# Six blocks of a sequence transform on two 64-row tiles of the array in place of the full 128 rows

## The chip, the cores and the metric

One core of a Trainium2 chip runs the kernel. The metric is the device time of one execution in microseconds. Three runs of the kernel before gave 882.68, 882.76 and 883.76 us, a median of 882.76 us. Operands are float32; a product is built up from rounded halves, as told below.

## The reference, cut to what matters

The input is a sequence of S = 2048 rows by D = 512. Two branches work on it, and a gate per row mixes them.

```
g = sigmoid((x * gate_w).sum(-1))
a = x @ dft_hid_re.T ;  b = x @ dft_hid_im.T
y = dft_seq_re @ a - dft_seq_im @ b                 # the sequence transform, 2048 x 2048 twice
o = windowed causal attention of x, 32 heads of 16, window 256
out = g * y + (1 - g) * (o @ wo)
```

The change lies in `y`, in its second half, the product with `dft_seq_im`.

## The kernel before, in words

**Precision.** The kernel keeps each operand of a large product as two tiles, `hi` (the value rounded to the format `F32R`) and `lo` (the rest, also `F32R`), and forms hi x hi, hi x lo and lo x hi (`TERMS`). A product of 128 x 128 weights with 128 x 512 data is therefore three matmuls, each with its own weights or its own data. The attention's value product, `pv` (L411), takes plain float32, and so do the two small products in `m_rows` and `l_rows` (L331, L343).

**The sequence transform.** `dense` is a generator that emits matmuls one by one. For each half (0 is the real one, 1 the imaginary one) and each block `tb` of 128 rows of the result it sums over 16 chunks of 128 rows of the sequence: 16 x 3 = 48 matmuls into one PSUM bank (`dc`, one of two banks of the pool `ps_d`). `c_block` (L447) runs such a block, and `c_chunk` (L442) emits the three matmuls of one chunk. The weights `w` are pieces of the transform's matrix, loaded as `raw` and split by VectorE into `hi` and `lo` (L82, L83); the data `ab` are the 16 tiles `big` of `a` or `b`. At the end of a block, `add_r` (L563 to L573) reads the first half's result `r` back, adds the bank times the gate on VectorE (L566), and, once the attention is over, calls `wo_block`.

**The output projection.** `wo_block` (L592) loads 128 rows of the attention's result, splits them (ScalarE L80 and VectorE L83), runs 12 matmuls (L604) into a bank `t` out of the four of `ps_a` (tag `st`), and adds that bank times 1 - g to `r` on VectorE (L606) ahead of the store of the output.

**The order.** TensorE runs in the order in which the code is written. During the attention, the main loop emits score and probability products and draws matmuls from `dense` between them (`fill`); the transform's blocks up to `tb` = 9 of the second half are emitted or begun that way. When the loop is over, `attention_done` loads `wo` and appends it to `FIN`, and `for _ in stream: pass` emits what is left. From there on each finished block calls `wo_block` twice, once for a block that was waiting and once for itself, so that six blocks of 48 transform matmuls (`tb` 10 to 15) alternate with 24 projection matmuls, and 48 projection matmuls stand at the end. The order on VectorE and ScalarE is set by a scheduler at build time.

**Tiles of the array.** A matmul whose output has 32 partitions runs on a tile of the array of 128 rows by 32 columns: that is so in `pv`, whose four products `p` go to four such tiles side by side, and in L331 and L343. The profile prints it as 128*32. All others run on 128*128.

Of the kernel before, what the change touches and what calls it, by code (L numbers as in the profile page):

```python
# [7 lines left out]
F32 = mybir.dt.float32  # L8
F32R = mybir.dt.float32r
AF = mybir.ActivationFunctionType  # L10
OP = mybir.AluOpType
# [3 lines left out]
P = 128  # L15
# [16 lines left out]
def fnet_window_mix(ctx: ExitStack, tc: tile.TileContext, xT, x, wqk, wv, wr, wi, cr, ci, wo, gw, out):  # L32
    nc = tc.nc
# [3 lines left out]
    st = ctx.enter_context(tc.tile_pool(name="st", bufs=3))  # L37
    ev = ctx.enter_context(tc.tile_pool(name="ev", bufs=5))
    at = ctx.enter_context(tc.tile_pool(name="at", bufs=2))
    ps_a = ctx.enter_context(tc.tile_pool(name="ps_a", bufs=4, space=PSUM))  # L40
    ps_o = ctx.enter_context(tc.tile_pool(name="ps_o", bufs=2, space=PSUM))
    ps_d = ctx.enter_context(tc.tile_pool(name="ps_d", bufs=2, space=PSUM))
# [11 lines left out]
    def ld(dst, src):  # L54
        return nc.sync.dma_start(dst, src)
# [38 lines left out]
    def load_raw(src):  # L94
        raw = st.tile([P, 1024], F32, name="raw", bufs=2)
        ld(raw, src)
        return raw

    def split_raw(raw, act=False):
        hi = st.tile([P, 1024], F32R, name="hi")  # L100
        lo = st.tile([P, 1024], F32R, name="lo")
        for c in HALVES:
            split(hi[:, c], lo[:, c], raw[:, c], act)
        return hi, lo
# [7 lines left out]
    def load_x(ss, j):  # L112
        raw = st.tile([P, 1024], F32, name="raw", bufs=2)
        ld(raw.rearrange("p (k s) -> p k s", k=2), xT[ss, 2 * j:2 * j + 2].rearrange("k p s -> p k s"))
        for c in range(2):
            XRAW[2 * j + c, ss] = raw[:, HALVES[c]]
# [41 lines left out]
    half = const.tile([P, 2], F32, name="half")  # L158
    mrow = const.tile([P, 2], F32, name="mrow")
    for t, edges in ((half, ((0, 16, 32, 48, 64, 80), (16, 32, 48, 64, 80, 96))), (mrow, ((96, 98), (98, 100)))):  # L160
        nc.gpsimd.memset(t, 0.0)
        for h in range(2):
            for i, e in enumerate(edges[h]):
                a = t[:, h:h + 1]
# [23 lines left out]
    g1 = const.tile([P, 16], F32, name="g1")  # L188
# [23 lines left out]
    TERMS = ((0, 0), (0, 1), (1, 0))  # L212
# [7 lines left out]
    def qk_first(w):  # L220
        pss = [ps_a.tile([P, 512], F32, name="s", tag="st") for _ in range(2)]
        for dk in range(DK):
            for i in range(2):
                c = dk * 256 + i * 128
                for n, (a, b) in enumerate(TERMS):
                    nc.tensor.matmul(pss[i], w[a][:, c:c + 128], XT[dk, 0][:, b],
                                     start=dk == 0 and n == 0, stop=dk == 3 and n == 2)
        for i in range(2):
            qk_evict(0, 0, i, pss[i])

    def qk_proj(g, ss, w):
        for i in range(2):
            ps = ps_d.tile([P, 512], F32, name="dqk", tag="d")
            n = 0
            for dk in range(DK):
                c = dk * 256 + i * 128
                for a, b in TERMS:
                    nc.tensor.matmul(ps, w[a][:, c:c + 128], XT[dk, ss][:, b],  # L238
                                     start=n == 0, stop=n == 11)
                    n += 1  # L240
                    if n < 12:
                        yield
            qk_evict(g, ss, i, ps)
            yield
# [21 lines left out]
    def v_proj(sb, w):  # L266
        ps = ps_d.tile([P, 512], F32, name="dv", tag="d")
        yield from row_proj(sb, w, ps)
        t = ev.tile([P, 512], F32, name="ev")
        mark("act", nc.scalar.copy(t, ps))  # L270
        store(v_scr[sb // 2][sb % 2].rearrange("r a g x -> r (a g x)"), t)
        yield
# [164 lines left out]
    SC = [*range(4, 16), *range(4)]  # L437

    def c_chunk(w, i, ab, ps):
        s8 = i % 8  # L440
        for a, b in TERMS:
            nc.tensor.matmul(ps, w[a][:, s8 * 128:(s8 + 1) * 128], ab[SC[i]][:, b],  # L442
                             start=i == 0 and a + b == 0, stop=i == 15 and a == 1)
            if i < 15 or a == 0:
                yield

    def c_block(get, half, tb, ab, done):  # L447
        ps = ps_d.tile([P, 512], F32, name="dc", tag="d")
        for i in range(16):
            if i % 8 == 0:  # L450
                w = get((half, tb * 2 + i // 8))
            yield from c_chunk(w, i, ab, ps)
        done(tb, ps)
        yield

    def c_pair(get, half, tb, ab, done, last=False):
# [18 lines left out]
    def late(fn, *args):  # L475
        with behind("act", "dve"):
            return fn(*args)

    def dense():
        wraw = [load_raw(wv[i]) for i in range(2)]  # L480
        qk_first(wq0)
        wvs = [split_raw(r, True) for r in wraw]
        load_x(1, 0)
        load_x(1, 1)
        yield
        for ss in range(4):
            if ss:
                yield from qk_proj(0, ss, wq0)
            for c in range(4):
                yield from v_proj(ss * 4 + c, wvs)  # L490
                have.add(("v", ss * 4 + c))
                if c == 1:
                    have.add(("qk", 0, ss))
                if ss < 3:
                    if c in (1, 2):
                        late(split_x, ss + 1, (2 * c - 2, 2 * c - 1), ss == 0)
                        if ss < 2:
                            load_x(ss + 2, c - 1)
                elif c == 0:
                    raw = load_raw(wqk[1])  # L500
                    wraw = [load_raw(wi[0])]
                elif c == 2:
                    w = late(split_raw, raw)
        for g in range(1, NG):
            for ss in range(4):
                yield from qk_proj(g, ss, w)
                have.add(("qk", g, ss))
                if g == 1:
                    if ss == 0:
                        wraw.append(load_raw(wi[1]))  # L510
                    elif ss < 3:
                        if ss == 1:
                            ws = []
                        ws.append(late(split_raw, wraw[ss - 1]))
                        if ss == 1:
                            raw = load_raw(wqk[2])
                        else:
                            gate_load(0)
                elif g == 2:
                    if ss == 0:  # L520
                        raw = load_raw(wqk[3])
                        wraw = [load_raw(wr[0])]
                    elif ss == 2:
                        nextw = late(split_raw, raw)
                        wraw.append(load_raw(wr[1]))
                elif ss in (0, 2):
                    if ss == 0:
                        ws = []
                    ws.append(late(split_raw, wraw[ss // 2]))
            if g == 1:  # L530
                for sb in range(16):
                    yield from ab_proj(1, sb, ws)
                    if sb == 1:
                        nextw = late(split_raw, raw)
                    if sb % 2 == 0 and sb < 14:
                        gate_load(sb // 2 + 1)
                    if sb % 2:
                        late(gate, sb - 1)
                        late(gate, sb)
            if g < 3:  # L540
                w = nextw
        ab = {}
        for sb in range(16):
            if sb >= 4:
                ab[sb] = big.tile([P, 2, 512], F32R, name="big")
            yield from ab_proj(0, sb, ws, ab.get(sb))
        for sc in range(4):
            ab[sc] = load_ab(0, sc)
        have.add("proj")
        def store_r(tb, ps):  # L550
            t = ev.tile([P, 512], F32, name="ev")
            nc.scalar.activation(t, ps, AF.Copy, scale=g1[:, tb:tb + 1])
            ld(r_scr[0][tb], t)

        get = c_pieces([*((0, k) for k in (*range(28), 28, 30, 29, 31)),
                        *((1, k) for k in (0, 2, 1, 3, *range(4, 32)))])
        for tb in range(14):
            yield from c_block(get, 0, tb, ab, store_r)
        yield from c_pair(get, 0, 14, ab, store_r, True)
        ab = nxt  # L560
        wait = []

        def add_r(tb, ps):  # L563
            r = ev.tile([P, 512], F32, name="ev")
            ld(r, r_scr[0][tb])
            nc.vector.scalar_tensor_tensor(r, ps, g1[:, tb:tb + 1], r, op0=OP.mult, op1=OP.add)  # L566
            if FIN:
                if wait:
                    wo_block(wait.pop(0))
                wo_block(tb, r)  # L570
            else:
                ld(r_scr[1][tb], r)
                wait.append(tb)  # L573

        yield from c_pair(get, 1, 0, ab, add_r)
        for tb in range(2, 16):
            yield from c_block(get, 1, tb, ab, add_r)
        while wait:
            wo_block(wait.pop(0))

    FIN = []
# [147 lines left out]
```

## Time and profile before

| What | Before |
|---|---|
| Runs, median (lowest to highest) | 882.76 us (882.68 to 883.76) |
| Span of the profiled execution, first to last instruction | 881.0 us |
| Between that span and the median of the runs | 1.76 us |
| Mean clock granted to TensorE | 0.998 of full |
| TensorE busy (matmuls) | 867.3 us |
| Matmuls of the transform (L442), all | 1536 |
| Projection matmuls (L604) | 192 |
| First of the six blocks behind the attention starts at | 772.51 us of the chain |

The profiled execution's own time is its span of 881.0 us with what lies around it; the page gives no other time for it, so the median of the runs stands for the whole. Times of rows are microseconds from the span's start. TensorE appears twice: PE is the matmuls, PEld the weight loads, which may run beside them. A matmul's record is longer than its share of the engine, since matmuls overlap: the pitch, from one start to the next, is what counts. In a row of the chain or the timeline stand the start, the length, the line, what is written and read, and how many instructions were merged.

### The profile page before, as it was taken

To read this page: it belongs to the slowest core of one execution; us is meant where nothing else is said; L and a number is where in the kernel's file an instruction comes from. 1 tells how busy PE (TensorE), PEld (TensorE's weight loads), DVE (VectorE), ACT (ScalarE), POOL (GpSimd) and SP (SyncE) were. 2 spreads that over 40 slices of the span, in tenths; PEclk is the share of its full clock that TensorE was granted. 3 is DMA by queue.
4 is the path that set the end of the run, shared out by engine and by line. 5 is a ranking of instruction groups with operands and counts; after the bars stand their busy time and mean duration, and the time that the engine had idled before them with its cause. 6 is when DMAs were issued, how large, how long until landed. Compare 5 with 4: busy or idle time off the path is not lost.

```text
span 881.0 us, 17206 instructions
## 1 busy us (share of the span) xinstructions
PE 867.3 (98%) x5184; PEld 690.6 (78%) x5184; DVE 604.8 (69%) x1965; ACT 590.3 (67%) x1794; POOL 384.9 (44%) x1069
## 2 busy tenths in 40 slices
PE   7999899999999999999999999999999999999998
PEld 5888677777777778787878787878777787788886
DVE  4688789777888678787877677778786433544342
ACT  5488789878889887888888878888786444101000
POOL 9100165554544446656456565745555665100000
PEclk9999999999999999999999999999999999999999
DMA  7877667675656126544444454469743424355453
GB/s 246 274 232 212 197 218 263 216 246 179 225 198 213 43 72 216 159 130 126 140 141 132 147 147 128 134 203 324 256 154 95 137 96 144 110 180 165 134 160 113
DMA packets 89822, 152.13 MB, mean 173 GB/s; under 512 B 26752, under 2 KB 35456, under 8 KB 89728
## 3 DMA queue, kind: packets, MB, share of 16 engines
q1 hardware_dynamic: 89728, 151.02, 54.6%
q8 instruction: 41, 0.67, 0.3%
q14 instruction: 53, 0.43, 0.2%
HBM read 103.81 MB, written 47.19 MB: 171 GB/s over the span
## 4 chain that ended last, share of the span: by engine, by line
PE 93%; DVE 2%; DMA 2%; ACT 1%; issue 0%; SPq 0%; ACTq 0%
PE dc L442 40%; PE s L319 9%; PE dab L260 9%; PE t L384 8%; PE dqk L238 8%; PE o L411 8%; PE t L604 5%; PE dv L260 5%; DMA qk_scr<-hl 1%; DMA pt<-xT 1%; DMA ab_scr<-hl 1%; DVE sm L321 1%; ACT sm L324 0%; PE s L343 0%; PE s L331 0%
## 5 line engine op out<-in xcount | busy, mean ns | idle before, releaser
L442 PE MATMUL dc<-big,hi 128*128 128x512 f32 x1024 | 341.0, 394 | 0.0
L390 POOL TENSOR_SCALAR_AFFINE_SELECT pt<-pt 64x128 f32<-64x128 f32 x512 | 195.4, 382 | 285.2 <-ACT pt L385 270.1
L321 DVE CUSTOM_DVE_ANT_0 sm<-s,mask 128x320 f32<-128x320 f32 (+4 forms) x512 | 232.6, 462 | 114.6 <-PE t L384 74.9
L324 ACT ACTIVATE sm<-sm,nm 128x320 f32<-128x320 f32 (+4 forms) x512 | 276.6, 541 | 25.8 <-DVE nm L321 21.7
L385 ACT ACTIVATE pt<-t 128x320 f32<-128x320 f32 (+4 forms) x512 | 210.8, 414 | 117.9 <-PE t L384 114.4
L442 PEld LDWEIGHTS dc<-big,hi 128*128 128x128 f32 x1024 | 189.4, 188 | 28.1
L442 PE MATMUL dc<-big,lo 128*128 128x512 f32 x512 | 201.6, 394 | 0.0
L384 PE MATMUL t<-ring,pad 128*128 128x320 f32 (+4 forms) x512 | 158.3, 309 | 3.8 <-ACT pad L302 2.8
L319 PE MATMUL s<-ring,pad 128*128 128x320 f32 (+4 forms) x512 | 160.4, 313 | 0.8 <-ACT pt L385 0.8
L394 POOL TENSOR_SCALAR_AFFINE_SELECT pt<-pt 64x128 f32<-64x128 f32 x448 | 157.1, 351 | 0.0
L304 DVE TENSOR_SCALAR pad<-ring,half 96x256 fp32r<-96x256 f32 x384 | 122.3, 365 | 27.4 <-PE t L384 26.2
L319 PEld LDWEIGHTS s<-ring,pad 128*128 128x128 f32 x512 | 96.2, 188 | 41.5 <-issue 7.4
L384 PEld LDWEIGHTS t<-ring,pad 128*128 128x128 f32 x512 | 96.4, 188 | 27.8 <-issue 3.2
L442 PEld LDWEIGHTS dc<-big,lo 128*128 128x128 f32 x512 | 96.3, 188 | 11.2
L83 DVE TENSOR_TENSOR lo<-raw,hi 128x512 fp32r<-128x512 f32 x146 | 99.5, 709 | 0.2 <-ACT hi L80 0.2
L324 ACT ACTIVATION_READ_ACCUMULATOR sm<-sm,nm 128x1 f32 x512 | 97.8, 191 | 0.0
L260 PE MATMUL dab<-hi,big 128*128 128x512 f32 x256 | 86.6, 395 | 0.2 <-DVE hl L88 0.2
L82 DVE CAST hi<-raw 128x512 fp32r<-128x512 f32 x142 | 57.8, 444 | 39.2 <-DMA raw<-ci 19.6
L238 PE MATMUL dqk<-big,hi 128*128 128x512 f32 x240 | 84.2, 398 | 0.0
L80 ACT CAST raw<-ev 128x512 fp32r<-128x512 f32 x16 | 9.9, 621 | 108.5 <-DVE lo L83 64.9
L411 PE MATMUL o<-pt,vpad 128*32 128x320 f32 (+4 forms) x1408 | 78.4, 352 | 0.0
L411 PEld LDWEIGHTS o<-pt,vpad 128*32 128x32 f32 x1408 | 35.9, 109 | 37.5 <-issue 18.0
(79 smaller groups left out, 823.4 us busy)
## 6 DMA issues: line engine op xcount, KB each, us to landing
qk_scr<-hl SPq DMA_DIRECT2D x32, 512.0 KB
ring<-qk_scr SPq DMA_DIRECT2D x32, 512.0 KB
raw<-cr SPq DMA_DIRECT2D x32, 512.0 KB
raw<-ci SPq DMA_DIRECT2D x32, 512.0 KB
ab_scr<-hl SPq DMA_DIRECT2D x20, 512.0 KB
big<-ab_scr SPq DMA_DIRECT2D x20, 512.0 KB
ring<-qk_scr SPq DMA_DIRECT2D x32, 256.0 KB
r_scr<-ev SPq DMA_DIRECT2D x25, 256.0 KB
```

The lines of the kernel that those rows point to most:

```text
L238: nc.tensor.matmul(ps, w[a][:, c:c + 128], XT[dk, ss][:, b], start=n == 0, stop=n == 11)
L260: nc.tensor.matmul(ps, XT[dk, ss][:, a, c * 128:(c + 1) * 128], wh[b], start=n == 0, stop=n == 11)
L304: nc.vector.tensor_scalar(dst, src, half[:96, h:h + 1], None, op0=OP.mult)
L319: nc.tensor.matmul(ps[:, :w], PAD[0, n][:, p], ring[1][:, p, k0:k0 + w], start=True, stop=True)
L321: mark("dve", nc.vector.tensor_tensor_reduce(out=sm[:, :w], in0=ps[:, :w], in1=mask[:, WIN - w:], scale=1.0, scalar=3e38, op0=OP.add, op1= ...
L324: mark("act", nc.scalar.activation(sm[:, :w], sm[:, :w], AF.Exp, bias=nm[:, c], scale=-1.0, accum_out=l[:, c]))
L384: nc.tensor.matmul(ps[:, :w], PAD[1, n][:, p], ring[0][:, p, q0:q0 + w], start=True, stop=True)
L385: nc.scalar.activation(pt[:, p, :w], ps[:, :w], AF.Exp, scale=-1.0)
L390: nc.gpsimd.affine_select(a, a, pattern=[[0, 2], [1, 64]], compare_op=OP.is_ge, fill=0.0, base=0, channel_multiplier=-1)
L394: nc.gpsimd.affine_select(a, a, pattern=[[0, 2], [-1, 64]], compare_op=OP.is_gt, fill=0.0, base=0, channel_multiplier=1)
L411: nc.tensor.matmul(OT[g, sb][32 * p:32 * p + 32, q - sb * 512:e - sb * 512], v2[:, p], pt[:, p, q - q0:e - q0], start=first, stop=kb == 8 ...
L442: nc.tensor.matmul(ps, w[a][:, s8 * 128:(s8 + 1) * 128], ab[SC[i]][:, b], start=i == 0 and a + b == 0, stop=i == 15 and a == 1)
```

## The change

When a block of the transform starts with the attention over (`FIN` not empty), `c_block` hands over to a new generator, `c_rows`. It emits the same chunks and terms, but each product as two matmuls: rows 0 to 63 of weights and data into one bank (`dc`, from `ps_d`), rows 64 to 127 into another (`dr`, from the four banks of `ps_a`). `add_r` takes both banks and adds them to `r` one after the other. This applies to the six blocks `tb` 10 to 15; the projection is unchanged.

```diff
     def c_block(get, half, tb, ab, done):
+        if FIN:
+            yield from c_rows(get, half, tb, ab, done)
+            return
         ps = ps_d.tile([P, 512], F32, name="dc", tag="d")
...
+    def c_rows(get, half, tb, ab, done):
+        ps = [ps_d.tile([P, 512], F32, name="dc", tag="d"), ps_a.tile([P, 512], F32, name="dr", tag="st")]
+        for i in range(16):
+            if i % 8 == 0:
+                w = get((half, tb * 2 + i // 8))
+            s8 = i % 8
+            for a, b in TERMS:
+                for h in range(2):
+                    r = slice(64 * h, 64 * h + 64)
+                    nc.tensor.matmul(ps[h], w[a][r, s8 * 128:(s8 + 1) * 128], ab[SC[i]][r, b],
+                                     start=i == 0 and a + b == 0, stop=i == 15 and a == 1)
+                if i < 15 or a == 0:
+                    yield
+        done(tb, *ps)
+        yield
...
-        def add_r(tb, ps):
+        def add_r(tb, *pss):
             r = ev.tile([P, 512], F32, name="ev")
             ld(r, r_scr[0][tb])
-            nc.vector.scalar_tensor_tensor(r, ps, g1[:, tb:tb + 1], r, op0=OP.mult, op1=OP.add)
+            for ps in pss:
+                nc.vector.scalar_tensor_tensor(r, ps, g1[:, tb:tb + 1], r, op0=OP.mult, op1=OP.add)
```

On TensorE, at the first projection behind the attention (`t` is its bank, `fin` the split `wo`, `raw` the split attention result), this stood before:

```order
L442 MATMUL dc<-big,hi 128x512 x2
L442 MATMUL dc<-big,lo 128x512
L604 MATMUL t<-fin,raw 128x512 x24
L442 MATMUL dc<-big,hi 128x512 x2
L442 MATMUL dc<-big,lo 128x512
```

And this stands at the same place now (the line numbers have grown by 20 there):

```order
L442 MATMUL dc<-big,hi 128x512 x2
L442 MATMUL dc<-big,lo 128x512
L624 MATMUL t<-fin,raw 128x512 x24
L468 MATMUL dc<-big,hi 128x512
L468 MATMUL dr<-big,hi 128x512
L468 MATMUL dc<-big,hi 128x512
L468 MATMUL dr<-big,hi 128x512
L468 MATMUL dc<-big,lo 128x512
L468 MATMUL dr<-big,lo 128x512
```

The three matmuls of a chunk have become six that alternate between the two banks; the rows' 128 is the output's partitions, the contraction is 64 rows each. All 288 matmuls of the six blocks become 576 in this way, and the 24 projection matmuls stand where they stood.

On VectorE, at the end of the first of the six blocks (`ev` is `r`, `g` the gate, `raw` the split of the attention's result for the next projection), the piece of the difference is this:

```order
 L83 TENSOR_TENSOR lo<-raw,hi 128x512
 L83 TENSOR_TENSOR raw<-ev,raw 128x512
-L566 SCALAR_TENSOR_TENSOR ev<-dc,g_314,ev 128x512
-L606 SCALAR_TENSOR_TENSOR ev<-t,g_315,ev 128x512
+L586 SCALAR_TENSOR_TENSOR ev<-dc,g_314,ev 128x512
+L586 SCALAR_TENSOR_TENSOR ev<-dr,g_314,ev 128x512
+L626 SCALAR_TENSOR_TENSOR ev<-t,g_315,ev 128x512
 L82 CAST hi<-raw 128x512
```

The addition of the second bank stands behind that of the first, ahead of the projection's addition; the splits around them have kept their places. On SyncE, ScalarE and GpSimd the order of instructions is that of before.

## The prediction

> **What bounds the kernel now.** I read the head of the page first, then the chain that ended last, then that chain in order of time over the last 125 us, where the change lies, and last the timelines at a block's edge.
>
> ```profile
> span 881.0 us, 17206 instructions
> PE 867.3 (98%) x5184; PEld 690.6 (78%) x5184; DVE 604.8 (69%) x1965; ACT 590.3 (67%) x1794; POOL 384.9 (44%) x1069
> PE 93%; DVE 2%; DMA 2%; ACT 1%; issue 0%; SPq 0%; ACTq 0%
> ```
>
> TensorE is busy 98% of the span and holds 93% of the chain: whatever TensorE saves or loses in the tail comes out at the end of the kernel. The chain in order of time (start, us, what) shows how the tail is put together:
>
> ```profile
> 761.92 4.99 PE dc L442 x21
> 766.92 5.60 PE t L604 x24
> 772.51 10.90 PE dc L442 x48
> ...
> 855.01 10.90 PE dc L442 x48
> 865.92 11.21 PE t L604 x48
> 877.12 0.02 issue
> 877.15 0.75 DVE ev L606
> ```
>
> From 761.92 the chain is TensorE alone, without a gap, until one VectorE operation and the last store. Six blocks of the sequence transform (48 matmuls each) alternate with two output-projection blocks each (24 matmuls); the first of the six starts at 772.51 and the last at 855.01. A transform matmul stands for 10.90 / 48 = 0.227 us, a projection matmul for 5.60 / 24 = 0.233 us, though both stream 512 columns. The six blocks hold 6 x 48 = 288 matmuls, and those 288 are what the change rewrites: 65.4 us of the span. So 1 ns on the pitch of a matmul (or of the pair that takes its place) is worth 0.29 us.
>
> The profile's span is 881.0 us and the median of the runs 882.76 us; the 1.76 us between them lie outside the span and I carry them along unchanged.
>
> **What the pitch is made of.** The timeline at the edge of a block (start, us, engine) has the weight loads beside the matmuls:
>
> ```profile
> 782.35 0.39 PE L442 MATMUL dc<-big,lo 128*128 128x512 f32 x1
> 782.35 0.41 PEld L442 LDWEIGHTS dc<-big,hi 128*128 128x128 f32 x2
> 782.57 0.62 PE L442 MATMUL dc<-big,hi 128*128 128x512 f32 x2
> 782.80 0.19 PEld L442 LDWEIGHTS dc<-big,lo 128*128 128x128 f32 x1
> 783.03 0.39 PE L442 MATMUL dc<-big,lo 128*128 128x512 f32 x1
> 783.25 5.76 PE L604 MATMUL t<-fin,raw 128*128 128x512 f32 x24
> 783.46 0.75 DVE L566 SCALAR_TENSOR_TENSOR ev<-dc,g,ev 128x512 f32<-128x512 f32 x1 [2.78 <-PE dc L442]
> ```
>
> Each matmul has its own weights, and the load for the next one starts in the same hundredth of a microsecond as the matmul before it (782.35 and 782.35). How long a load really holds the array's weight port shows where a matmul is too short to cover it, a 64-column one early in the attention:
>
> ```profile
> 34.80 0.39 PE L260 MATMUL dv<-hi,big 128*128 128x512 f32 x1
> 35.02 0.19 PE L319 MATMUL s<-ring,pad 128*128 128x64 f32 x1
> 35.02 0.19 PEld L260 LDWEIGHTS dv<-lo,big 128*128 128x128 f32 x1
> 35.05 0.47 PE L260 MATMUL dv<-lo,big 128*128 128x512 f32 x1
> 35.13 0.19 PEld L260 LDWEIGHTS dv<-hi,big 128*128 128x128 f32 x1
> ```
>
> The matmul of 35.05 lasts 0.47 us and not 0.39, and the load behind it begins only at 35.13: the load of 35.02 took 0.11 us, and 0.08 us of it was waited for. Under a 512-column matmul these 0.11 us are covered.
>
> **The change, part by part.** (1) *The stream.* Each matmul of 128 rows by 512 columns becomes two of 64 rows by 512 columns, into two banks. Nothing gets shorter by itself: each half streams all 512 columns of its 64 rows. So the question is whether the halves run at the same time. Nothing in the kernel before runs on row tiles, but the attention's value product runs on tiles of 32 columns. The groups by form in one stretch of it (how many of each, us together, mean ns of one | idle):
>
> ```profile
> L411 PE MATMUL o<-pt,vpad 128*32 128x320 f32 x8 | 0.7, 445 | 0.0
> L411 PE MATMUL o<-pt,vpad 128*32 128x256 f32 x8 | 0.6, 379 | 0.0
> L411 PE MATMUL o<-pt,vpad 128*32 128x64 f32 x8 | 0.3, 219 | 0.0
> ```
>
> The chain around that stretch, with full-array matmuls of 320 columns (L384) before and after:
>
> ```profile
> 705.88 0.15 PE t L384
> ...
> 708.82 1.22 PE o L411 x24
> 710.03 0.34 PE t L384
> ```
>
> And the timeline of lone 128-column products which, like the value product, take plain float32 (the transform's operands are the rounded kind):
>
> ```profile
> 681.80 0.38 PE L331 MATMUL s<-ident,nm 128*32 128x128 f32 x2
> 682.02 0.38 PE L343 MATMUL s<-ident,l 128*32 128x128 f32 x2
> ```
>
> Two lone products need 682.02 - 681.80 = 0.22 us for 256 columns, 0.86 ns a column. The 24 matmuls stream 8 x (320 + 256 + 64) = 5120 columns, which at that rate would be 4.4 us; they took 1.22. So the four tiles did run at once. I take it that two row tiles do too, and that the pair's pitch is that of the matmul it replaces: 288 x 0 = **0 us**. The ends by the nearest rows: 0.22 us (34.80 to 35.02, the shortest pitch of a 512-column matmul quoted) gives 288 x -0.007 = -2.0 us; 0.233 us (the projection) gives +1.8; two streams one after the other give 288 x 0.227 = +65.4. I take 0 because 0.227 is measured on these operands in this stretch. The Trainium skill, "TensorE: Matmul & The Clock Gate", Part 3, Measured speedup vs the span model, adds about 4 ns for each further tile; if that were added to every pair it would be 288 x 4 ns = 1.2 us and the total 886.3. The trace cannot separate so little.
>
> (2) *The loads.* Two per pair in place of one, each still 128 columns wide. At 0.11 us each, one after the other, they need 0.22 us, and 0.227 is there to cover them: **0 us**, with a cover of only 7 ns. If they do not fit, see the rival.
>
> (3) *Changing between tiles and the full array.* Twelve times: into and out of each of the six blocks, since the projection stays on the full array. The way in stands in the timeline ahead of the same value product:
>
> ```profile
> 708.20 0.39 PE L442 MATMUL dc<-big,lo 128*128 128x512 f32 x1
> 708.43 0.39 PE L442 MATMUL dc<-big,hi 128*128 128x512 f32 x1
> 708.75 0.48 PE L411 MATMUL o<-pt,vpad 128*32 128x320 f32 x4
> ```
>
> Going in, the pitch was 708.75 - 708.43 = 0.32 us where 0.23 stood before: 0.09 us late, and there the load is not covered; a load of 128 columns adds its 0.11. That is 0.20 us. Coming out, by the chain's rows above, the first full-array matmul (710.03) takes 0.34 us where its like (705.88) takes 0.15: 0.19 us, the uncovered load in it. 6 x 0.20 + 6 x 0.19 = **+2.3 us**. Ends: 12 x 0.09 = 1.1 if the loads stay covered, and 6 x 0.31 + 6 x 0.19 = 3.0 if both tiles' first loads come one after the other.
>
> (4) *The second addition.* Six more VectorE operations of 0.75 us (the row of 783.46 above). In the last block:
>
> ```profile
> 865.96 0.75 DVE L566 SCALAR_TENSOR_TENSOR ev<-dc,g,ev 128x512 f32<-128x512 f32 x1 [4.61 <-PE dc L442]
> 868.75 0.75 DVE L606 SCALAR_TENSOR_TENSOR ev<-t,g,ev 128x512 f32<-128x512 f32 x1 [2.05 <-PE t L604]
> 869.45 0.69 DVE L83 TENSOR_TENSOR raw<-ev,raw 128x512 fp32r<-128x512 f32 x1
> ```
>
> Behind the first addition VectorE waits 2.05 us for the projection; the second fits in there. The splits that the next projections need stand ahead of both additions on VectorE, or behind this gap. The cover is the 2.8 us of twelve projection matmuls (5.60 / 2); without it, six times 0.75 us would be at most 4.5. I cost it at **0**.
>
> (5) *The second bank* comes from the four that the projections rotate through. With three takers a round in place of two, a block's second bank was last read one block earlier (10.90 us), and a reader holds it 0.75 us. **0**. SyncE, the loads of coefficients and the work ahead of 772.51 are in the order of before.
>
> Sum: 881.0 + 0 + 0 + 2.3 + 0 + 0 = 883.3 us of span, and with 1.76 outside it **885.1 us**.
>
> **The rivals.** *The tiles do not run together*, and the split does not do what it says. The column tiles speak against it; but they share their rows and split the output, and here it is the other way round, for which the trace has no row. 882.76 + 65.4 + 2.3 = 950.5 us. Chance 0.12.
>
> *No load ahead on a tile*: each half must end before its next weights go in. Then each pair pays the 0.11 us: 288 x 0.11 = 31.7, and 882.76 + 31.7 + 2.3 = 916.8 us. Against it stand the rows of 782.35, where the load starts with a matmul of the same rows. The Trainium skill, "TensorE: Matmul & The Clock Gate", Part 3, The mechanism, has such a rule: a load overlaps a running matmul only if it goes to another row group. By that rule the loads of 782.35 could not stand where they do; the trace disagrees for the full array, and for row tiles it has no row. Chance 0.06.
>
> *The weight port becomes the bound.* The 0.11 us was measured while the stream stood still; a load that competes with a stream and costs 0.12 to 0.125 us makes the pair 0.24 to 0.25: 288 x (0.013 to 0.023) = 3.7 to 6.6 us, and with 2.3 to 3.0 for the switches 889 to 892, say 890.5 us. For it: only 7 ns of cover. Against it, the groups of the weight loads between 708.74 and 708.77:
>
> ```profile
> L411 PEld LDWEIGHTS o<-pt,vpad 128*32 128x32 f32 x4 | 0.1, 106 | 0.4 <-POOL pt L390 0.4
> ```
>
> Four loads of column tiles were under way within 0.03 us and took 0.1 us together, no longer than one: they went in side by side. Chance 0.17.
>
> *Faster*: some of a pitch is not streaming but the exchange of weights. A 320-column matmul stands for 0.15 us (705.88 above) and a 512-column one for 0.227: 0.40 ns a column, so 512 columns would be 0.205, and 0.022 us of each pitch do not scale. If one tile streams while the other exchanges, up to 288 x 0.022 = 6.3 us are saved; half of that is 3.2, and 882.76 - 3.2 + 2.3 = 881.9; all of it, 878.8. It decides the sign from 2.3 / 288 = 8 ns a pair. I take the middle, 880.5 us. Against it: the two halves start together and exchange together. Chance 0.10.
>
> **How the numbers follow.** The forecast, 885.1 us, has 0.55; its own range is 883.9 (switches at 1.1) to 888 (pitch 0.233, switches 3.0, a little more). A measurement of this kernel can tell about 0.2%, 1.8 us, from no change, so "same" ends at 884.5. The range reaches down to most of the faster case and up to the end of the weight port's: 880.0 to 893.0; out are the two far cases (0.18) and little else. Slower by over 0.2%: the far cases 0.18, the port 0.17 and most of the forecast, 0.41: 0.76. Same: 0.14 of the forecast and 0.05 of the faster case: 0.19. Faster by over 0.2%: the rest of that case, 0.05.
>
> **What would show it.** In the profile after, the chain's row of a block's 96 tile matmuls should last about 11.1 us for the 10.90 of before, and the projections 5.8 for 5.60. Two matmuls that start within 0.01 us, then 0.227 us until the next two, show the tiles at work; even steps of 0.23 show them in line. A pair at 0.24 or more with loads back to back is the port; 0.33 is the load that does not go ahead. The prediction is wrong if VectorE or a bank appears as a releaser of TensorE after 772.

## The result, and the profile after

The changed kernel takes 885.51 us (median of 6 runs, 883.88 to 886.72), the kernel before 882.86 us (6 runs, 881.25 to 883.76). The ratio is 1.0031, 95% interval 1.0016 to 1.0045: slower by 0.3%, which the interval keeps clear of no change. The profiled execution took 885.39 us, of which 883.7 are its span.

The head of the page after, and its shares of the chain by engine:

```profile
span 883.7 us, 17794 instructions
PE 870.0 (98%) x5472; PEld 693.0 (78%) x5472; DVE 609.6 (69%) x1971; ACT 590.7 (67%) x1794; POOL 385.2 (44%) x1069
PE 94%; DMA 3%; DVE 2%; ACT 1%; issue 0%; SPq 0%; ACTq 0%
```

TensorE has 288 matmuls more and its busy time only 2.7 us more. The chain of the tail in order of time (start, us, what), in three stretches:

```profile
767.08 5.60 PE t L624 x24
772.68 0.43 PE dc L468
```

```profile
783.56 0.21 PE dc L468
783.78 0.01 PE dr L468
783.79 5.80 PE t L624 x24
```

```profile
868.39 11.40 PE t L624 x48
879.78 0.02 issue
879.81 0.75 DVE ev L626
```

The first tile block lasts from 772.68 to 783.79, 11.11 us for the 10.90 of a block before, and the projection behind it 5.80 for 5.60. The first tile step stands for 0.43 us in place of 0.23, because it holds one whole change. From the first projection to the last, 767.08 to 879.78, it is 112.70 us, and before (766.92 to 877.12) 110.20: **2.5 us** more, in twelve pieces of 0.2. The timeline (start, us) shows the inside of a block first and then its edge. Inside:

```profile
776.82 0.39 PE L468 MATMUL dc<-big,hi 64*128 64x512 f32 x1
776.83 0.39 PE L468 MATMUL dr<-big,hi 64*128 64x512 f32 x1
777.05 0.39 PE L468 MATMUL dc<-big,hi 64*128 64x512 f32 x1
777.05 0.18 PEld L468 LDWEIGHTS dc<-big,lo 64*128 64x128 f32 x1
777.06 0.39 PE L468 MATMUL dr<-big,hi 64*128 64x512 f32 x1
777.06 0.18 PEld L468 LDWEIGHTS dr<-big,lo 64*128 64x128 f32 x1
777.27 0.39 PE L468 MATMUL dc<-big,lo 64*128 64x512 f32 x1
```

The two halves start 0.01 us apart, the next pair 0.23 us later; and each load starts with the matmul of its own tile. The edge:

```profile
771.59 1.10 PE L624 MATMUL t<-fin,raw 128*128 128x512 f32 x4
...
772.61 0.18 PEld L468 LDWEIGHTS dc<-big,hi 64*128 64x128 f32 x1 [0.37 <-issue]
772.61 0.50 PE L468 MATMUL dc<-big,hi 64*128 64x512 f32 x1
772.62 0.18 PEld L468 LDWEIGHTS dr<-big,hi 64*128 64x128 f32 x1
772.62 0.72 PE L468 MATMUL dr<-big,hi 64*128 64x512 f32 x2
...
772.72 0.19 PEld L468 LDWEIGHTS dc<-big,hi 64*128 64x128 f32 x1
772.72 0.19 PEld L468 LDWEIGHTS dr<-big,hi 64*128 64x128 f32 x1
...
772.96 0.39 PE L468 MATMUL dc<-big,hi 64*128 64x512 f32 x1
```

The last of the four projection matmuls starts three steps of 0.233 us behind 771.59, at 772.29; the block starts 0.32 us later where a step is 0.23, a standstill of 0.09 us. The first matmul of the block is 0.50 us long instead of 0.39, and both tiles' second loads begin at 772.72: the two first loads took 0.11 us together and were waited for, so the next pair comes at 772.96, 0.35 us behind the first. The loads' engine stood idle ahead of them for a reason that no semaphore explains ("issue"). The view of waits for the tail counts these places (us in total, times, longest):

```profile
PEld dc L468 <- issue: 2.2, 6, 0.4
PEld t L624 <- issue: 2.1, 6, 0.4
```

Six and six: the twelve changes between tiles and full array. In this profile TensorE and its loads wait for no other engine in the tail. In some profiles below, and in that of the same kernel run once more (c0), a load in the last projection block waits for the split of that block; this adds between 0.05 us (e2) and 0.5 us (e1) to their tails, 0.1 us in c0.

A word on what can be compared. The work ahead of the tail is the same in all these kernels, but their profiles reach the first projection at 764 to 768 us. Below, "the tail" is therefore the time from the start of the first projection matmul to that of the last, within one profile: 109.96 us before and 112.46 us after the change, the same difference of 2.5. A change of the array's division right ahead of the first projection matmul has its standstill of 0.09 us outside the tail; that is so in e1 and e9.

### The profile page after: what moved, and what is told of

Read it like the earlier page. It is cut to its first block, busy times and chain, and to the rows that moved or that the text cites. A ratio compares the mean times of both kernels' runs of the same rounds, so it can differ in the third digit from the quotient of the medians.

```text
span 883.7 us, 17794 instructions
## 1 busy us (share of the span) xinstructions
PE 870.0 (98%) x5472; PEld 693.0 (78%) x5472; DVE 609.6 (69%) x1971; ACT 590.7 (67%) x1794; POOL 385.2 (44%) x1069
## 4 chain that ended last, share of the span: by engine, by line
PE 94%; DMA 3%; DVE 2%; ACT 1%; issue 0%; SPq 0%; ACTq 0%
PE dc L442 33%; PE s L319 9%; PE dqk L238 8%; PE t L384 8%; PE o L411 8%; PE dab L260 8%; PE dc L468 7%; PE t L624 5%; PE dv L260 5%; DMA ab_scr<-hl 1%; PE s L226 1%; DMA qk_scr<-hl 1%; DVE sm L321 1%; PE dr L468 0%; ACT sm L324 0%
## 5 line engine op out<-in xcount | busy, mean ns | idle before, releaser
L442 PE MATMUL dc<-big,hi 128*128 128x512 f32 x832 | 281.8, 395 | 0.0
L442 PEld LDWEIGHTS dc<-big,hi 128*128 128x128 f32 x832 | 153.3, 188 | 20.4
L442 PE MATMUL dc<-big,lo 128*128 128x512 f32 x416 | 164.3, 395 | 0.0
L442 PEld LDWEIGHTS dc<-big,lo 128*128 128x128 f32 x416 | 78.3, 188 | 7.5
```

## The experiments

**The change once more** (c0), beside the first three experiments on one chip. 

> The changed kernel once more, on the same chip as the next three, as their measure. Every theory expects 885.5 us, within 1.5.

 Measured: 884.69 us (9 runs), 882.10 for the kernel before (24 runs), ratio 1.0027 (1.0016 to 1.0038); tail 112.57 us. The result stands; 0.1 us of the tail is the wait named above.

**The projection on tiles too** (e1).

```diff
-        ps = ps_a.tile([P, 512], F32, name="t", tag="st")
+        k = P // (1 + rows)
+        pss = [ps_a.tile([P, 512], F32, name="t", tag="st") for _ in range(1 + rows)]
...
-                nc.tensor.matmul(ps, o[:, a, g], FIN[0][:, g // 2, g % 2, b], start=n == 0, stop=n == 11)
+                for h, ps in enumerate(pss):
+                    q = slice(k * h, k * h + k)
+                    nc.tensor.matmul(ps, o[q, a, g], FIN[0][q, g // 2, g % 2, b], start=n == 0, stop=n == 11)
...
-            wo_block(wait.pop(0))
+            wo_block(wait.pop(0), rows=False)
```

> The projection behind the attention also runs on the two row tiles, all but its last two blocks; the second bank is added by one more VectorE operation per block. Instead of 12 changes between tiles and full array there are 2. Theory (the cost is the 12 changes at 0.195 us): 885.5 - 10 x 0.195 = 883.6 us if a projection pair keeps its 0.233 us; 1.0 less, 882.6, if it takes 0.227. Rival (each pair of half matmuls costs 2.65 / 288 = 9 ns more than the matmul it replaces, wherever it runs): 168 more pairs, 885.5 + 1.5 = 887.0 us.

 Measured: 883.64 us (11 runs), ratio to before 1.0012 (1.0003 to 1.0021); tail 110.81 us. The tail is 1.65 us shorter than that of the change, where the rival has it 1.5 longer. The time is 1.05 us under the 884.69 of c0, about half of the 1.95 that the theory has; that it meets the theory's 883.6 is luck, since c0 is itself 0.8 under 885.5. The tail is 0.85 us over that of before, and two changes make 0.31 of it (0.40 less the 0.09 outside). The chain of its end has the other 0.54:

```profile
867.40 8.59 PE t L627 x60
876.00 0.02 issue
876.02 3.34 PE t L627 x12
```

Its last twelve matmuls take 3.34 us, not 2.80. The loads in its timeline say why:

```profile
876.01 0.30 PEld L627 LDWEIGHTS t<-fin,raw 128*128 128x128 f32 x2 [0.45 <-ACT raw L80]
876.74 2.16 PEld L627 LDWEIGHTS t<-fin,raw 128*128 128x128 f32 x10 [0.43 <-DVE raw L83]
```

They waited for the splits of the last block on ScalarE and VectorE. In both kernels the data of that block is sent for 0.6 us behind a store of the output (870.17 behind 869.53 before, 872.47 behind 871.87 here). That store now stands behind two additions (870.24, 1.61 us) in place of one (868.75, 0.75). So the likely reason is the second addition; it was not tried alone.

**The same, with the end left alone** (e9): the last four projection blocks stay on the full array, `rows=tb < 15` in `add_r`. 

> The projection on row tiles again, but now the last four of its blocks (behind the sixth transform block) stay on the full array, so that the end of the kernel is that of before. 2 changes instead of 12. Theory (0.2 us for each change, nothing else, and the wait at the end of the last run came from the later release of buffers there): the stretch from the first projection matmul to the last matmul 110.0 + 2 x 0.2 = 110.4 us, where the kernel before has 109.96 and the change 112.46; a time 0.4 us over that of before, which cannot be told from no change. Rival (the tiles bring costs of their own): 111 us or more, 1 us over before.

 Measured: 882.47 us (12 runs) against 882.02 (17 runs), ratio 1.0001 (0.9992 to 1.0009). The first change and the last block in its profile:

```profile
766.34 0.39 PE L442 MATMUL dc<-big,lo 128*128 128x512 f32 x1
766.65 0.50 PE L627 MATMUL t<-fin,raw 64*128 64x512 f32 x2
...
874.80 2.16 PEld L627 LDWEIGHTS t<-fin,raw 128*128 128x128 f32 x10 [0.24 <-DVE raw L83]
```

The tail is 110.35 us, 0.39 over that of before and as expected to 0.05, but in part by luck, for two small errors cancel. The first change's standstill (766.34 to 766.65, 0.32 us in place of 0.23) lies ahead of the tail, so the two changes make 0.31 of the 0.39; the other 0.08 is the wait of one load for VectorE at 874.80. Counted from the matmul ahead of the tail it is 0.48 us: two changes of 0.20 and that wait. The 288 pairs of the transform and 144 of the projection on tiles cost nothing. With ten of the twelve changes gone, the times show no loss any more.

**More changes** (e3): odd chunks on the full array, into the first bank.

```diff
+            if i % 2:
+                for a, b in TERMS:
+                    nc.tensor.matmul(ps[0], w[a][:, s8 * 128:(s8 + 1) * 128], ab[SC[i]][:, b],
+                                     start=False, stop=i == 15 and a == 1)
...
+                continue
```

> In the six blocks only the even chunks run on two row tiles; the odd ones run on the full array, into the first bank. 96 changes between tiles and full array instead of 12, and half as many pairs. Theory (each change 0.2 us): the changed kernel + 84 x 0.2 = 16.8 us, about 901.5 us. Rival (a cost per pair, 9 ns): half of the 2.6 us goes, about 883.5 us.

 Measured: 903.34 us (4 runs) against 882.02, ratio 1.0237 (1.0220 to 1.0253); tail 130.47 us. Fewer pairs and a much longer time: (130.47 - 109.96) / 96 = 0.214 us a change. The rival, a cost per pair, is out.

**Tiles of two sizes** (e8): odd chunks on four tiles of 32 rows (`k = 32 if i % 2 else 64`, four banks). 

> Even chunks on two tiles of 64 rows, odd chunks on four tiles of 32 rows: 17 changes of the array's division per block, 102 in all, only 12 of them from or to the full array. Theory (every change of the division costs the 0.2 us): 885 + 90 x 0.2 = 903 us. Rival (only leaving or entering the full array costs): 885 us.

 Measured: 905.04 us (2 runs), ratio 1.0258 (1.0237 to 1.0279); tail 132.19 us. (132.19 - 109.96) / 102 = 0.218 us. A change from one tile size to another cost here what a change to the full array cost in e3. In its timeline:

```profile
775.21 0.39 PE L470 MATMUL dc<-big,lo 32*128 32x512 f32 x1
775.21 0.40 PE L470 MATMUL dr<-big,lo 32*128 32x512 f32 x3
775.54 0.50 PE L470 MATMUL dc<-big,hi 64*128 64x512 f32 x1
775.54 0.50 PE L470 MATMUL dr<-big,hi 64*128 64x512 f32 x1
775.88 0.39 PE L470 MATMUL dc<-big,hi 64*128 64x512 f32 x1
```

775.21 to 775.54 is 0.33, 0.10 late, and 775.54 to 775.88 is 0.34, where 0.23 is the step: the 0.11 us of an uncovered load.

**Four tiles** (e5): `range(4)`, slices of 32 rows, three banks of `ps_a` beside `dc`. 

> Four tiles of 32 rows and four banks in place of two of 64: 1152 half-size matmuls in four streams, four weight loads of 128 columns per step, four additions per block. Theory (tiles stream at once, loads go in side by side, 12 changes as before): 885.5 to 887 us, a step of 0.227 us. Rival (the weight port takes one load after the other, 0.11 us each, and two only just fitted): 0.44 us a step, 885.5 + 288 x 0.213 = 947 us.

 Measured: 884.66 us (6 runs), 884.69 for the change beside it, ratio to before 1.0027 (1.0016 to 1.0038); tail 112.75 us, about 0.2 of it the wait at the end.

```profile
775.02 0.38 PE L469 MATMUL dc<-big,hi 32*128 32x512 f32 x1
775.03 0.41 PE L469 MATMUL dr<-big,hi 32*128 32x512 f32 x3
775.25 0.38 PE L469 MATMUL dc<-big,lo 32*128 32x512 f32 x1
775.25 0.18 PEld L469 LDWEIGHTS dc<-big,hi 32*128 32x128 f32 x1
775.25 0.41 PE L469 MATMUL dr<-big,lo 32*128 32x512 f32 x3
775.26 0.21 PEld L469 LDWEIGHTS dr<-big,hi 32*128 32x128 f32 x3
775.47 0.38 PE L469 MATMUL dc<-big,hi 32*128 32x512 f32 x1
```

Four matmuls, each with its load of 128 columns, start every 0.225 us. One after the other, four loads of 0.11 us would need 0.44. So the loads of different row tiles went in side by side.

**Without the second addition** (e4): `for ps in pss[:1]`. 

> The six additions of the second bank are left out, and with them the share of rows 64 to 127 of the contraction in the last six blocks of the output. Theory (they are covered by the projection): 885.5 us, within 0.5 of the changed kernel. Rival (the additions are what the change costs, up to 6 x 0.75 = 4.5 us): 881.0 to 883 us.

 Measured: 884.65 us (7 runs), 884.69 for the change beside it; tail 112.47 us. No cost of the additions can be seen.

**One tile after the other** (e2).

```diff
-            for a, b in TERMS:
-                for h in range(2):
-                    r = slice(64 * h, 64 * h + 64)
+            for h in range(2):
+                r = slice(64 * h, 64 * h + 64)
+                for s8 in range(8):
+                    i = 8 * j + s8
+                    for a, b in TERMS:
```

> The same half matmuls in another order: for each piece of weights first 24 on rows 0 to 63, then 24 on rows 64 to 127. Theory (two tiles stream together only where their matmuls stand next to each other in the order; alone, half a matmul takes the 0.227 us of a whole one): 576 - 18 = 558 steps of 0.227 for 288, + 61 us, about 946 us. Rival (TensorE finds work for the free tile by itself in the matmuls that it holds): down to 885 us.

 Measured: 936.41 us (2 runs), ratio 1.0614 (1.0593 to 1.0635); tail 164.21 us. Theory and rival were both wrong by some way, the theory by 10 us. A turn from one tile to the other in its timeline:

```profile
776.35 0.39 PE L468 MATMUL dc<-big,lo 64*128 64x512 f32 x1
776.35 0.49 PE L468 MATMUL dr<-big,hi 64*128 64x512 f32 x1
776.57 0.39 PE L468 MATMUL dc<-big,hi 64*128 64x512 f32 x1
776.69 0.39 PE L468 MATMUL dr<-big,hi 64*128 64x512 f32 x1
776.80 0.39 PE L468 MATMUL dc<-big,hi 64*128 64x512 f32 x1
776.92 0.39 PE L468 MATMUL dr<-big,lo 64*128 64x512 f32 x1
777.02 0.39 PE L468 MATMUL dc<-big,lo 64*128 64x512 f32 x1
```

In the program all 24 `dc` stand ahead of the first `dr`. On the chip the first `dr` starts at 776.35, with three `dc` (776.57, 776.80, 777.02) still to come. A block lasts 19.73 us from its first start to the projection's, not the 21.98 of 96 steps of 0.227 and a change: 2.25 us or ten steps are saved at its three turns, 3.3 at each, where I had counted one. TensorE started matmuls for a free tile out of turn, but not far ahead. Two more runs test how far.

**Six and six, twelve and twelve** (e10, e11): the same with 2 and with 4 chunks of one tile before the other's turn.

```diff
+            if i % 2:
+                continue
+            for h in range(2):
+                r = slice(64 * h, 64 * h + 64)
+                for k in range(i, i + 2):
```

> As the run with 24 and 24, but 6 half matmuls on rows 0 to 63 and then 6 on rows 64 to 127. In the run with 24 and 24 each turn from one tile to the other saved 3.3 steps of 0.227 us. Theory (TensorE starts matmuls for a free tile out of turn, past about three others): two turns save 6.7 of 12 steps, so 6 and 6 run side by side as in the changed kernel, about 885 us. Rival (strictly in order, one step saved at a turn): 10 of 12 steps remain, 288 x 10/6 x 0.227, about 929 us.

 Measured: 889.15 us (3 runs) against 882.75 (4 runs), ratio 1.0074 (1.0051 to 1.0097); tail 116.53 us. The theory was 4 us short. A block takes 11.79 us for the 11.12 of the changed kernel, 0.67 or three steps more: three steps at its start (its first `dc` at 771.52, its first `dr` at 772.10 beside the third `dc`) and three at its end (three `dr` from 782.55) in which one tile works alone. Between them the tiles keep up with each other; the rival's 929 us is out.

> The same with 12 and 12. Theory: 24 - 6.7 = 17.3 steps where the changed kernel has 12, so 24 x 5.3 x 0.227 = 29 us more, about 914 us. Rival (in order): 22 steps, 24 x 10 x 0.227 = 54 us more, about 940 us. If the reach were 12 or more: 885 us.

 Measured: 918.73 us (2 runs), ratio 1.0405 (1.0375 to 1.0435); tail 145.67 us. The theory said 914, the rival 940. The theory took off 3.3 steps for eight turns a block, and there are seven; a step of 0.227 us, 3.3 times in six blocks, is 4.5 us of the 4.7 it missed. With seven, 96 - 23 = 73 steps make 16.6 us a block, and the profile has 16.65. A reach of about three matmuls past those that wait fits all three runs, and none fits a strict order. Whether the limit counts matmuls, loads or something else was not tried.

## Why the prediction was right

It was right in time (885.1 for 885.51, interval of the ratio 1.0016 to 1.0045 against 1.0027 forecast) and in its terms, one of them for a reason other than mine; I take them by their numbers. That the medians meet within 0.4 us is closer than the scatter of the runs (883.88 to 886.72) allows to expect; the tail is the better measure.

(1) *The stream*, 0 us: the pairs' step is that of the matmul before (776.82, 777.05, 777.27), and 432 pairs in e9 left a tail that two changes and a wait of 0.08 us explain. That it rests on two tiles working at once is shown by e2, where the same matmuls in another order cost 54.4 us over before. The inference from the column tiles held. One reading in it was off: the row of 681.80 is one plain float32 product in two instructions and not two products, for L331 has 32 matmuls in the profile for its 16 products; the columns counted are the same.

(2) *The loads*, 0 us: right, but for another reason. I had one load after the other with 7 ns to spare; in the change's own rows the two loads run together (777.05 and 777.06), and e5 has four side by side. So the 0 was lucky as far as my reason goes. The rival of the weight port had 0.17 and was the likeliest; it could have had less on the row of four column loads in 0.1 us.

(3) *The changes*, +2.3 us: measured 2.5, 0.209 us each for 0.195. The same two parts were in the timeline as forecast: 0.09 to 0.10 us of standstill and 0.11 us of uncovered load. I had read both parts on the way in and put the way out down to the load alone; in the changed kernel both stand there as well (the last pair at 783.39, the projection at 783.72, 0.10 late). e3 gives 0.214 a change, e8 0.218, e9 0.20. The upper end, two first loads in line, did not occur: they shared 0.11 us (772.61 to 772.72). The Trainium skill, "TensorEngine Tiling (Array Packing)", Key Properties, says that a change of the tiling mode drains TensorE; the runs agree, and put 0.10 us on the standstill and 0.21 on the whole.

(4) *The second addition*, 0 us: e4 is level with the change (884.65 and 884.69). (5) *The second bank*, 0 us: in the profile of the change no bank and no engine appears among what TensorE waited for. In c0 VectorE does appear, which I had named as a sign of being wrong: one load of the last projection block waits for a split, at a cost of 0.1 us, which is no part of the 2.5. Neither the second addition nor the second bank is what it waits for, and what delays the split in some profiles and not in others stays open.

The rivals: tiles in line would have been 950.5 us; no load ahead, 916.8, is out by the rows of 777.05 and 777.06, where the load starts with its own tile's matmul. The Trainium skill, "TensorE: Matmul & The Clock Gate", Part 3, The mechanism, says in one place that a load overlaps a running matmul only in another row group, and in another that a load into a background weight buffer goes ahead too. The trace disagrees with the first for row tiles as it did for the full array, and is at one with the second; the prediction had taken up the first alone. The faster case needed 8 ns a pair and got none that can be seen.

The medians of the first comparison lie 2.65 us apart and the tails 2.50; what is left is within the scatter of the work ahead of the tail, which is the same program.

## What to carry to other kernels

Splitting a contraction that already fills the array gained nothing here: two half-height tiles at once did the work of one 512-column matmul in its 0.227 us. What is paid is every change of the array's division, about 0.21 us here, so count the changes between products and keep neighbours on one division. The order of the matmuls decides whether tiles work together: put those of different tiles next to each other.

## What the runs showed of the hardware that was not expected

TensorE did not start matmuls strictly in the order of the program when they went to different row tiles: at 776.35 in e2 it took one from behind three others. The words ahead of the prediction, that TensorE runs in the order in which the code is written, hold for the order of the instructions and not for these starts. The Trainium skill, "TensorE: Matmul & The Clock Gate", Part 3, The mechanism, says that matmuls start in the program's order without reordering; here they do not, and the time agrees with the records: e2 is 10 us faster than a strict order with one step saved at each turn would make it.

A projection matmul stands for 0.233 us and a transform matmul for 0.227, on the full array and on tiles alike; in the chain of e9 the 24 pairs of two projection blocks take the 5.60 us that 24 matmuls took before:

```profile
783.42 5.60 PE t L627 x48
```

What sets these 3% apart was not tried.
